# A block-sorted attention with a Fourier-mix layer: another order on all engines, one more pair of identity matmuls, and a buffer's clear on GpSimd

## The chip, the cores and the metric

The kernel runs on one core of a Trainium2 chip. A core has five instruction streams: PE (TensorE, matmuls and the weight loads PEld that go with them), DVE (VectorE), ACT (ScalarE), POOL (GpSimd) and SP (SyncE, which here only issues DMAs). They wait for each other through semaphores. The metric is device time in microseconds (us). Three runs of the kernel before gave 272.65 us in the median (271.55, 272.65, 272.99). The profile is of a further execution: 271.9 us as timed, with a span of 270.1 us from its first to its last instruction.

## The reference, cut to what matters

There are four batches of 8 heads, 768 positions and head size 64. For each head an 8x8 matrix is made doubly stochastic in five rounds, and mixes the eight 96-row blocks of K and V. Block-local attention follows. Its output, reshaped to 768x512 per batch, goes through a 2-D Fourier transform of which the real part is kept, a residual, a normalization and a two-layer MLP with 2048 hidden units.

```python
P = sort_net
for _ in range(5):
    P = np.exp(P - max(P, -1)); P = P / sum(P, -1); P = P / sum(P, -2)
k_sorted = einsum('bhij,bhjcd->bhicd', P, k_b); v_sorted = einsum(..., P, v_b)
scores = scale * q_b @ k_sorted.T          # inside each of the 8 blocks
attn = softmax(scores); x = attn @ v_sorted
u = x + real(fft2(x))                      # per batch, 768 x 512
un = (u - mean(u)) / sqrt(var(u) + 1e-6)
out = u + relu(un @ w_ch1) @ w_ch2
```

## The kernel before, in words

The program is cut into small steps, written as generators `t_<letter>`. A long string, `ORDER`, is a list of tokens; each token runs one generator up to its next `yield`. At the end every instruction of PE, DVE, ACT, SP and POOL is tied to the one before it on the same engine. So the string fixes the order on each engine, and only semaphores decide when an instruction starts. A second string, `SLOTS`, gives one digit to each buffer that is taken in that order: which of eight PSUM banks, or which copy of a rotating SBUF tile.

A token's letter names the step and its digits the batch, head pair, tile or column group. A trailing A or D says whether ACT or DVE empties PSUM, and a P or D whether POOL or DVE does an addition. The steps that matter here, with their lines:

- `M`: matmuls with the identity that sum V over the block rows (L425). `Z`: the mean from them (DVE L432, L437). `s`: V minus its mean, six DVE operations per V load (L463). `v`, `w`: V mixed by the stochastic matrix (L476, L486), copied out by ACT or DVE (L286, L288).
- `J`, `D`: the stochastic matrix spread over partitions by PE (L389, L448). `B`, `T`, `b`: its block-diagonal forms (DVE L398, L410, L452).
- `q`: Q transposed, for batches 0 and 1 by PE (L306), for 2 and 3 by a crossbar transfer: a DVE copy into the single buffer `qr` (L297), then a DMA transpose from SP (L300). `k`: K mixed (PE L511) and copied to one of two `ksb` buffers.
- `x`: scores (PE L529) and exp (ACT L534). `e`: exp minus 1 into one of four score buffers `ebuf` (DVE L548). `o`: attention times V (PE L561), reciprocal and product (DVE L570, L575).
- `a`, `A`, `R`, `r`: a correction for the means, to small tables (PE L583, L608, L615; ACT L627; DVE L636).
- `f`, `c`, `d`, `p`: the Fourier transform (DVE L680 to L707, PE L719, PE L755 and L758, DVE L769, ACT L776, POOL L782 and L784). `g`, `l`, `n`: normalization (DVE L791 and L795, POOL L799 to L808, ACT L816 or DVE L819), transposed by PE (L830) in batch 0 and by a DMA transpose (L825) in the others.
- `h`: first MLP layer (PE L843, relu by ACT L852 or DVE L850). `y`: second layer (PE L863), residual (DVE L868), output from SP (L870).
- `C`, `L`, `V`: loads. `C0` is a constant table, its copy into `vcx` by POOL (L357), then four loads of w1 (L362) and four of w2 (L365). `L20`, `L21`, `L30`, `L31` load Q, then K, of half a batch's heads (L188). `V` loads the second half of V (L229). All but the tables are issued by POOL, in its order.
- `I`: two 128x512 matmuls with the identity whose result nobody reads (L277), which wait for a given round of the stochastic iteration.

Ahead of the string come, in program order: the first loads from POOL (two of V, then Q, K, Q, K of batch 0), clears of buffers, and `load_next`, which loads Q and K of batch 1 (L203). Three of the four `ebuf` buffers are cleared by DVE (L246), the fourth by POOL (L258). The five rounds of the stochastic iteration (L316 to L324) run on DVE and ACT.

Of the kernel before, what the change touches and what calls it, by code (L numbers as in the profile page):

```python
# [18 lines left out]
H = 8  # L19
S = 768  # L20
D = 64  # L21
# [85 lines left out]
def kernel(  # L107
# [10 lines left out]
    nc = tc.nc  # L118
# [7 lines left out]
        "00011101 00010234 50671030 12436570 13541602 05240031 63725241 "  # L126
        "61012052 63475001 25314102 06103012 04513222 10030415 11274602 "
        "53130145 36510210 03210302 01560420 33200075 60111221 22340330 "
        "01276225 10173200 00200653 04210013 13610004 56102525 11621110 "
        "65112701 35471623 05243052 00016450 16110470 21112364 21160323 "  # L130
        "61172420 61372041 64161010 20345245 17630010 04176325 11271652 "
        "37261401 05032102 33560171 00310010 00620057 32036401 11017624 "
        "23213156 23520605 43101204 47051106 01110521 03411070 16502411 "
        "02713260 50732415 00274113 52224760 11003511 22104731 00001210 "
        "17315000 14236220 31041230 03107652 01103651 01547162 30400762 "
        "37631401 07521240 11101501 01641320 27614031 54302100 11023201 "
        "50262732 36000054 07001001 51143120 04353542 00117102 16572110 "
        "40111035 60270456 07453147 352041 "
# [27 lines left out]
    def start(ins):  # L166
        return tc.keep_in_program_order(ins)
# [74 lines left out]
    NE = 4  # L242
    eb4 = const.tile([97, NE, 2 * S], F16, name="eb4")
    ebuf = [eb4[:, n, :] for n in range(NE)]
    for n in range(NE - 1):
        nc.vector.memset(ebuf[n][0:96, :], 0.0)  # L246
# [11 lines left out]
    start(nc.gpsimd.memset(ebuf[NE - 1][0:96, :], 0.0))  # L258
# [621 lines left out]
    def t_i():  # L880
        idle_mm(1)
# [3 lines left out]
        "C0 I4 I5 M00 M01 M02 M03 J M04 M05 C0 B0 C1 B1 B2 D q00A Z0 "  # L885
        "Z0 s02 k00AA H k01AD Z0 s03 q00 k00 k00 k00 x001 k01 b0 s01 "
        "x000 x001 s04 b0 x000 x000 a0 a0 x001 s05 s00 q01D k01 q02D "
        "k01 k02AA q01 e001 k02 k02 v61A v61 v40A e001 v70A v40 v41D "
        "v50D a0 b1 k02 v41 q02 v30A v30 x010 V x010 x010 V T1 v70 "
        "v20A e010 v20 v50 e000 e000 e010 A0 R0 x011 x021 R0 R0 R0 "  # L890
        "q03D q03 R0 R0 x011 x011 x021 v60D v10A v60 v00A k10AA v10 "
        "e011 e011 x021 k03AA R0 v00 x020 x020 k03 k03 k03 o00 o01 "
        "k10 k10 k10 x020 e021 x030 o00 e020 x030 x030 e021 o02 o01 "
        "o00 o01 o03 o02 o03 x031 q11A r1 C2 C3 r0 r1 e030 o03 e020 "
        "o04 k11AA x031 e031 x031 o05 e030 R0 o04 e031 o04 q11 k11 R0 "
        "o02 o05 k11 q10A q13A q13 v51A o07 o07 o05 q10 v51 M10 o06 "
        "v31A k11 x111 x101 x101 x101 v31 M11 o07 o06 f00 o06 f00 "
        "v21A v01A f01 f01 k13AA e101 x110 f02 k13 f02 M12 M13 e101 "
        "f03 f03 M14 v21 x100 x111 x110 x111 e110 c00 L20 f04 x100 "
        "x110 c00 b1 L30 M15 C0 L20 q20 C0 f05 f05 Z1 v01 C0 e111 "  # L900
        "e110 c01 c01 c02 c00 e111 c01 c02 c03 c04 e100 r0 r0 v71A "
        "k12AA c03 q20 c04 d02 v71 v11A x100 d02 p02P d00 p02 d01 k12 "
        "q12A k12 e100 d00 c03 p00P p01P q12 v11 k13 d02 c04 d00 d01 "
        "Z1 c02 d04 p00 k12 k13 d01 p02 p01 p01 p04P Z1 I1 p00 d05 T2 "
        "g02 g01 p05P x121 x121 x131 x131 a1 o13 o10 a1 x121 g00 g01 "
        "x131 C0 g02 g00 l00 l00 l00 l00 e121 o12 I2 x130 e131 o11 "
        "d04 o12 d05 x130 x130 d05 d04 k20AA n001AA o11 q21 I3 e130 "
        "o11 d03 n001 n002AA n001 L21 n000DD o16 n002 p04 o12 n000 "
        "n000 L21 C0 p04 o16 p05 C0 n002 x120 x120 d03 k20 e130 p03P "
        "o13 s15 e120 o13 h00iA h00fD h00f h00i x120 o10 s10 o10 "  # L910
        "h00jD h00j e121 d03 h00cA h00pA h00hA h00h h00p q21 o16 "
        "h00dA e120 k21AA k21 s13 k21 k20 k20 h00c h00kD e131 s12 s14 "
        "x200 k21 h00oA h00nA s11 o14 x200 h00d x200 h00gA o17 h00aA "
        "h00k h00a h00lA wpA h00g p05 C0 o17 o17 o15 h00mA h00bA g05 "
        "o15 o14 o14 wkA h00l h00b wk h00n h00eA h00e o15 f10 h00o wp "
        "y0010 y0020 e200 g04 x201 x201 L30 x211 x211 p03 p03 g03 f11 "
        "f11 g04 f10 f12 h00m C0 g05 g03 l01 f12 e200 f13 y0021 y0022 "
        "l01 l01 x201 weD wbA wb wgD c10 we y0023 l01 q22 f13 n011DA "
        "e201 c10 f14 woA c11 c11 wo y0000 wjD e211 wj x211 y0001 "
        "n011 n011 c12 wg f15 whA wdA y0011 y0002 c13 c12 wh y0023 "  # L920
        "y0023 r1 n012DD f15 n012 y0012 wlA n012 c13 y0013 wcA q22 "
        "wnD waA wa n010DD n010 wl y0003 n010 wd c14 c14 h01aA wn "
        "y0003 wfD q23 q23 T3 y0013 c10 d11 h01oA h01o wiA h01dD h01d "
        "h01lA h01l y0003 y0013 d10 h01pA wc h01a wi h01p wf h01jD "
        "wmD h01gA wm e201 x210 d10 d10 c11 h01g x210 x210 p10P h01j "
        "d12 h01mA k22AD k22 k22 k22 e210 e210 k23DD q31 k23 k23 "
        "h01cA c13 d11 p12P h01c h01hA h01h p11P k23 h01fA h01f e211 "
        "h01iA d12 h01bD d12 p11 h01m h01i h01kA x230 x231 d11 h01b "
        "p12 p12 p11 g11 g12 g11 g12 x220 h01eA x230 h01e x220 x230 "
        "y0110 o22 x231 e231 o20 h01nD h01n o20 h01k o21 p10 p10 o23 "  # L930
        "o23 o20 L31 x220 L31 g10 g10 o23 y0111 y0112 y0120 a1 l10 "
        "l10 l10 l10 o22 o22 y0121 k31AA c14 n101A k31 q31 e230 e220 "
        "A1 c12 x231 o21 o21 k31 x221 n101 R1 e231 R1 n100A n100 "
        "y0100 y0101 q30 R1 R1 R1 n102A n102 x221 y0113 y0113 d13 "
        "y0102 y0122 R1 R1 e230 y0113 x221 e221 k31 d14 R1 R1 r2 r2 "
        "h10iA h10nA h10i d14 q30 k30DD e221 k30 k30 k30 y0123 r2 "
        "e220 y0123 p14P o27 h10eD h10n h10e h10kD o27 d14 y0123 "
        "y0103 d15 o27 h10aA h10a h10dA h10gA h10g h10bA y0103 h10k "
        "p13D p15P h10cA h10c h10hA h10mA h10m h10d q32 d13 d13 y0103 "
        "h10lA h10h h10jD p13 p14 p14 g14 d15 d15 g14 p15 p15 h10fA "  # L940
        "h10f h10oA o26 g15 p13 g13 g13 g15 l11 l11 l11 h10j o26 "
        "h10pD o26 h10b y1010 l11 o24 o24 y1000 h10l o25 n110D o25 "
        "h10o h10p y1011 x311 x311 x311 x301 f21 o25 f21 y1001 n112A "
        "x301 y1020 y1021 o24 f20 f20 n110 r3 e301 n111D y1002 y1012 "
        "f22 f22 f23 f23 c20 c20 y1013 y1022 q32 x300 x301 x300 x310 "
        "y1023 c21 c21 n112 f24 f25 c23 n111 e311 q33 y1013 y1023 c23 "
        "h11cD c22 f25 y1003 y1003 y1023 y1003 c22 c24 x300 h11c c24 "
        "k32DD k33DA k33 k33 e311 x310 k32 k32 d21 k33 p21P k32 d21 "
        "d21 e300 h11fD h11f h11oA e310 d22 d20 p20P h11lA p22P d22 "
        "d22 c24 h11mA c20 r3 h11kA q33 y1013 d20 h11l h11o p22 p22 "  # L950
        "h11m x310 h11hD h11jA h11j g22 o32 x331 e300 x331 h11bA p21 "
        "h11h x331 h11k g22 o32 h11eA h11iA e310 p20 c23 e301 p21 g21 "
        "h11b o32 h11pD h11aD h11a h11e h11i d20 p20 g20 g20 e331 "
        "x330 g21 l20 l20 l20 l20 h11p x321 h11gA h11g h11dA o31 x321 "
        "o30 o31 o31 e321 x321 h11nA h11d n202A y1110 x330 c22 o33 "
        "h11n y1111 y1112 n202 o33 e330 e331 c21 n201A o33 n201 n200D "
        "n200 r3 y1100 y1101 e321 x320 x320 e320 y1113 y1113 o30 "
        "y1120 x320 x330 e330 y1102 y1103 y1121 y1122 y1123 y1103 "
        "h20nA h20aA h20dD h20a d24 p24P y1123 y1123 d24 d24 d23 h20n "
        "h20lD h20l h20pD h20kD p23P h20k o30 h20jA h20j y1103 d25 "  # L960
        "d25 p24 p24 p25P g24 h20fD h20f h20p h20cA h20iD y1113 o34 "
        "h20c h20bA h20b h20eD d23 d23 d25 h20d p23 e320 h20mD o35 "
        "o35 h20i p25 p25 g25 o35 h20gA o37 h20hA p23 g23 g23 h20oA "
        "h20h h20g g25 h20e o36 o36 g24 l21 l21 l21 o36 l21 n210A "
        "h20o h20m o34 o37 o34 f30 f30 o37 y2020 y2010 y2021 y2022 "
        "y2011 f32 y2023 n210 y2012 y2013 f31 f31 f32 f33 f33 n212D "
# [75 lines left out]
```

## Time and profile before

| | busy us | share of the 270.1 us span | instructions |
|---|---|---|---|
| PE | 251.8 | 93% | 2440 |
| DVE | 196.3 | 73% | 489 |
| ACT | 126.0 | 47% | 287 |
| POOL | 75.0 | 28% | 118 |

The span is the measure to which durations of the trace are added up. A busy time is the union of an engine's instructions, so an engine can be busy and still be waiting in a part of the run where another engine sets the pace. Matmuls overlap, so that the mean of one (326 ns for 128x384) is longer than its share of PE's time (0.65 us for four of them in the chain of waits). The first MLP matmul (L843) starts at 61.84 us, and the last matmul of the second layer ends shortly before 267.4 us.

### The profile page before, as it was taken

What the parts mean: (1) busy time and instruction counts of PE and PEld (TensorE: products, weight loads), DVE (VectorE), ACT (ScalarE), POOL (GpSimd) and SP (SyncE); (2) the same over time, 40 slices, a digit from 0 to 9 for tenths busy, and PEclk for the clock granted to TensorE, in tenths of its full rate; (3) what the DMA queues carried; (4) which work ended last, traced back from release to release, by engine and by line L of the source; (5) the groups of instructions that cost most, each with busy time, mean ns of one, the idle gap of its engine ahead of it and who ended that gap; (6) DMA issues with size and microseconds to landing.
All of it is one profiled execution on the core that took longest, in us unless ns stands there. A gap on an engine that the chain in (4) does not pass through costs nothing.

```text
span 270.1 us, 6119 instructions
## 1 busy us (share of the span) xinstructions
PE 251.8 (93%) x2440; PEld 156.0 (58%) x2440; DVE 196.3 (73%) x489; ACT 126.0 (47%) x287; POOL 75.0 (28%) x118
## 2 busy tenths in 40 slices
PE   0789889789999999999999999999999999999995
PEld 0268776565666666655656655466466545545554
DVE  6787999989999677867698696458965825912523
ACT  2268889885575477352633555133314312431100
POOL 8922400578730006402220053024200521410000
PEclk9988999999999999999999999999999999999999
DMA  6999999989971231843022310230023023020006
GB/s 120 203 253 203 221 245 235 181 104 178 204 119 39 45 102 29 119 107 101 15 55 52 94 47 12 55 119 1 19 42 116 0 45 132 0 53 8 0 12 223
DMA packets 33138, 26.38 MB, mean 98 GB/s; under 512 B 17395, under 2 KB 28787, under 8 KB 33108
## 3 DMA queue, kind: packets, MB, share of 16 engines
q0 software_dynamic: 11712, 13.63, 30.4%
q1 hardware_dynamic: 21398, 12.36, 17.2%
q8 instruction: 19, 0.31, 0.5%
q14 instruction: 9, 0.07, 0.1%
HBM read 29.00 MB, written 6.29 MB: 131 GB/s over the span
## 4 chain that ended last, share of the span: by engine, by line
PE 77%; DVE 8%; DMA 8%; POOL 2%; ACT 2%; issue 1%; DVEq 0%; SPq 0%; POOLq 0%
PE pf L863 31%; PE pf L843 27%; DMA k<-in_k_dram 6%; PE pf L719 3%; PE pf L561 3%; PE pf L529 2%; DVE eb L548 2%; DMA out_dram<-u 2%; PE pf L755 2%; PE pf L758 1%; DVE u L769 1%; PE pf L486 1%; PE pf L511 1%; PE pf L476 1%; PE pf L615 1%
## 5 line engine op out<-in xcount | busy, mean ns | idle before, releaser
L843 PE MATMUL pf<-ut,w1sb 128*128 128x384 f16 x512 | 89.9, 326 | 0.4 <-DVE hr L850 0.2
L863 PE MATMUL pf<-w2sb,hr 128*128 128x512 f16 (+1 forms) x432 | 88.6, 355 | 0.0
L843 PEld LDWEIGHTS <-w1sb 128*128 128x128 f16 x512 | 48.7, 98 | 31.5 <-issue 0.4
L852 ACT ACTIVATE hr<-pf 128x384 f16<-128x384 f32 x78 | 35.8, 494 | 60.6 <-PE pf L843 60.5
L863 PEld LDWEIGHTS <-hr 128*128 128x128 f16 x432 | 38.5, 98 | 37.7
L782 POOL TENSOR_TENSOR u<-u,bs 128x255 f32<-128x255 f32 x21 | 17.6, 844 | 120.2 <-ACT bs L776 69.1
L868 DVE TENSOR_TENSOR u<-pf,u 128x512 f32<-128x512 f32 (+1 forms) x27 | 17.0, 628 | 29.0 <-PE pf L863 28.9
L534 ACT ACTIVATE ex<-pf 96x384 f32<-96x384 f32 x64 | 28.8, 490 | 10.6 <-PE pf L529 8.0
L850 DVE TENSOR_SCALAR hr<-pf 128x384 f16<-128x384 f32 x50 | 26.3, 547 | 7.7 <-PE pf L843 7.6
L548 DVE TENSOR_SCALAR eb<-ex 96x384 f16<-96x384 f32 x64 | 22.9, 374 | 2.6 <-ACT ex L534 2.4
L769 DVE SCALAR_TENSOR_TENSOR u<-r,pf 128x256 f32<-128x256 f16 x48 | 18.3, 411 | 6.6 <-ACT bs L776 3.2
L784 POOL TENSOR_TENSOR u<-u,bs 128x255 f32<-128x255 f32 x21 | 17.7, 849 | 6.5 <-DVE u L769 6.4
L816 ACT ACTIVATE un<-u,nm,ny 128x512 f16<-128x512 f32 x14 | 11.1, 810 | 17.2 <-POOL nm L808 13.5
L791 DVE BATCH_NORM_STATS2 st<-u 128x6 f32<-128x512 f32 x24 | 16.3, 688 | 3.5 <-POOL u L784 3.1
L286 ACT CAST vsf<-pf 96x512 f16<-96x512 f32 x23 | 16.4, 741 | 3.1 <-PE pf L486 3.1
L575 DVE TENSOR_TENSOR r<-pf,rz 128x384 f16<-128x384 f32 x32 | 17.3, 547 | 0.2
L561 PEld LDWEIGHTS <-eb 97*128 97x128 f16 x384 | 14.9, 97 | 3.7 <-DVE eb L548 0.5
L561 PE MATMUL pf<-vsf,eb 97*128 97x65 f16 x384 | 16.4, 194 | 0.3 <-ACT ex L534 0.2
L733 ACT ACTIVATE y<-pf 128x386 f16<-128x386 f32 x16 | 7.4, 498 | 11.3 <-PE pf L719 11.3
L529 PE MATMUL pf<-qt,ksb 64*128 64x96 f16 x256 | 10.0, 209 | 2.5 <-ACT ksb L286 1.9
L277 PE MATMUL pf<-pack 128*128 128x512 f16 x12 | 4.4, 458 | 8.4 <-DVE pw L324 8.2
L286 ACT CAST ksb<-pf 128x384 f16<-128x384 f32 x23 | 10.5, 484 | 2.3 <-PE pf L511 1.6
(118 smaller groups left out, 302.8 us busy)
## 6 DMA issues: line engine op xcount, KB each, us to landing
out_dram<-u SPq DMA_DIRECT2D x23, 256.0 KB, 2.3
vst<-in_v_dram POOLq DMA_DIRECT2D x4, 768.0 KB, 11.7
q<-in_q_dram POOLq DMA_DIRECT2D x6, 384.0 KB, 13.2
k<-in_k_dram POOLq DMA_DIRECT2D x6, 384.0 KB, 10.6
w1sb<-in_moe_w_ch_dram POOLq DMA_DIRECT2D x4, 512.0 KB, 18.6
w2sb<-in_moe_w_ch_dram POOLq DMA_DIRECT2D x4, 512.0 KB, 8.1
kq<-in_k_dram POOLq DMA_DIRECT2D x2, 384.0 KB, 15.1
kq<-in_q_dram POOLq DMA_DIRECT2D x2, 384.0 KB, 16.2
```

Source lines behind the costliest of these rows:

```text
L286: nc.scalar.copy(dst, src)
L534: nc.scalar.activation(ex.rearrange("p j (c r) -> p j c r", r=6), pss[h2][0:96].rearrange("p j (r c) -> p j c r", c=16), AF.Exp, scale=SCALE)
L548: nc.vector.tensor_scalar(ed, exs[b, hp, g, h2], -1.0, None, op0=ALU.add)
L561: nc.tensor.matmul(po[:, 65 * T:65 * T + 65], e[:, S * g + 256 * tt + 128 * n: S * g + 256 * tt + 128 * n + 128], vsf[:, vi:vi + D + 1], s ...
L575: nc.vector.tensor_tensor(rt[:, :, D * h:D * h + D], po3[:, :, 0:D], rz[:, :, None].broadcast_to([128, 6, D]), op=ALU.mult)
L769: nc.vector.scalar_tensor_tensor(u[:, o:o + 256].rearrange("p (j n) -> p j n", n=2), rts[b][:, T, o:o + 256].rearrange("p (j n) -> p j n", ...
L782: e.tensor_tensor(u[:, 1:256], u[:, 1:256], bs[:, 1:256], op=ALU.add)
L784: e.tensor_tensor(u[:, 257:512], u[:, 257:512], bs[:, 255:0:-1], op=ALU.subtract)
L843: nc.tensor.matmul(ps, w1sb[:, c, 128 * fc:128 * fc + 128], uns[b, g][:, c, :], start=(c == 0), stop=(c == 3))
L850: nc.vector.tensor_scalar(hr[:, fc, :], ps, 0.0, None, op0=ALU.max)
L852: nc.scalar.activation(hr[:, fc, :], ps, AF.Relu)
L863: nc.tensor.matmul(po, hrs[b, g][:, fc, 128 * tt:128 * tt + 128], w2sb[:, fc, cols], start=(fc == 0), stop=(fc == 15))
```

## The change

The order string is written anew, with the same steps in it and one more token, and the string of buffer digits with it. Seen by engine:

- POOL clears two of the four `ebuf` buffers and DVE two, instead of one and three.
- A new step `t_F` takes the place of `t_i`, which no token used. It issues two identity matmuls with no wait of their own. One token `F6` runs it, on PE between the correction step `a0` and the first K mixing. The tokens `I1` to `I5`, two matmuls each as before, stand at other places.
- PE begins with `M00` instead of `I4 I5`. DVE begins with the mean and the six subtractions of V, ahead of the block-diagonal forms.
- POOL's order of loads was: table copy, V, V, L20 (Q), L30 (Q), w1, L20 (K), w1, w1, then w1, L21 and w2 between POOL's additions and normalization steps. It becomes: table copy, V, w1, L20 (Q), V, w1, w1, L20 (K), w1, w2, and later w2, L30 (Q), w2, w2, L30 (K), L21 (Q), L21 (K). The DMA transposes of Q for batch 2 (`q20`, `q21`) come later and the other way round on SP.
- Some PSUM copies change engine. Over the program, ACT has 89 instead of 78 of the 128 relus, 28 instead of 23 of the 32 `ksb` copies and 7 instead of 10 of the 16 copies of `w`. DVE has 6 instead of 3 of the 24 pairs of additions of `p`, and 15 instead of 13 of the 30 normalizing operations and first-batch copies of `n`.

```diff
     SLOTS = (
-        "00011101 00010234 50671030 12436570 13541602 05240031 63725241 "
+        "00011101 01112340 56016704 56301701 25620421 73530212 01041030 "
...
-    for n in range(NE - 1):
+    for n in range(NE - 2):
         nc.vector.memset(ebuf[n][0:96, :], 0.0)
...
-    start(nc.gpsimd.memset(ebuf[NE - 1][0:96, :], 0.0))
+    for n in (NE - 2, NE - 1):
+        start(nc.gpsimd.memset(ebuf[n][0:96, :], 0.0))
...
-    def t_i():
-        idle_mm(1)
+    def t_F(n):
+        idle_mm(2)
...
     ORDER = (
-        "C0 I4 I5 M00 M01 M02 M03 J M04 M05 C0 B0 C1 B1 B2 D q00A Z0 "
-        "Z0 s02 k00AA H k01AD Z0 s03 q00 k00 k00 k00 x001 k01 b0 s01 "
-        "x000 x001 s04 b0 x000 x000 a0 a0 x001 s05 s00 q01D k01 q02D "
-        "k01 k02AA q01 e001 k02 k02 v61A v61 v40A e001 v70A v40 v41D "
-        "v50D a0 b1 k02 v41 q02 v30A v30 x010 V x010 x010 V T1 v70 "
...
+        "C0 M00 M01 I3 M02 M03 M04 I4 M05 J Z0 Z0 H Z0 s05 D s01 s00 "
+        "C1 q00D q01A b0 s03 B1 s02 s04 a0 F6 q00 q01 b0 a0 k01AA k01 "
+        "k01 B0 B2 b1 v50A v50 k01 v61D v40A v60D v41D v40 k00AA k00 "
+        "v60 x011 v61 x011 x011 k00 x010 x010 k00 v41 q03D k03AD q03 "
+        "x001 x000 e010 k03 x001 k03 v30D e011 e011 a0 k03 x000 x010 "
+        "e010 x000 e000 e001 x001 C0 e001 e000 v20A v70A V C0 v00A "
+        "v00 v70 v10A v20 A0 v30 T1 v10 x031 R0 x031 x031 R0 L20 V C0 "
+        "x030 o02 R0 R0 C0 L20 C0 C0 R0 o02 R0 x030 o03 o03 e031 e031 "
...
-        "o11 d03 n001 n002AA n001 L21 n000DD o16 n002 p04 o12 n000 "
-        "n000 L21 C0 p04 o16 p05 C0 n002 x120 x120 d03 k20 e130 p03P "
-        "o13 s15 e120 o13 h00iA h00fD h00f h00i x120 o10 s10 o10 "
...
+        "x120 l00 x121 l00 d04 p05P o12 o11 k20AA k20 d03 o12 k20 k20 "
+        "d03 o11 n002DA o11 o10 M15 Z1 p05 C0 n002 o10 n001AD n001 "
+        "o13 n000AA n002 n000 n000 n001 x130 o10 e131 q21 e131 k21DA "
+        "k21 k21 k21 x121 p03 p03 Z1 e120 L30 h00hA h00oA g03 p05 "
...
-        "y3103 y3122 y3123 y3123 y3123 I6 "
+        "I6 y3123 y3123 "
```

## The prediction

> **What bounds the kernel now.** I read the page's head first, then the busy time by stage with the granted clock, then the waits of PE, then the first 25 us in order of time. The head:
>
> ```profile
> span 270.1 us, 6119 instructions
> PE 251.8 (93%) x2440; PEld 156.0 (58%) x2440; DVE 196.3 (73%) x489; ACT 126.0 (47%) x287; POOL 75.0 (28%) x118
> ```
>
> PE is nearly full, but the mean hides two stages. The table by stage gives for each stretch its length, each engine's busy time with its instructions, the granted clock, the DMA share and GB/s:
>
> ```profile
> 11.60:18.40 6.80, 5.41 (x64) 3.67 (x62) 6.14 (x16) 4.01 (x9) 2.31 (x4) 1.00 1.29 228
> 18.40:21.80 3.40, 3.29 (x48) 2.71 (x48) 1.79 (x4) 2.93 (x10) 2.93 (x4) 0.50 1.23 252
> 21.80:25.00 3.20, 2.67 (x73) 2.47 (x74) 2.41 (x8) 2.21 (x5) 0.11 (x1) 0.99 1.31 203
> 25.00:30.00 5.00, 4.75 (x91) 4.35 (x91) 4.73 (x12) 4.61 (x12) 1.12 (x2) 1.00 1.29 216
> 30.00:61.84 31.84, 27.37 (x499) 20.14 (x494) 30.77 (x87) 27.78 (x67) 12.37 (x19) 1.00 1.05 190
> 61.84:267.40 205.56, 204.95 (x1672) 121.71 (x1671) 142.45 (x337) 81.86 (x183) 45.67 (x70) 1.00 0.31 69
> ```
>
> From the first MLP matmul (61.84 us) to the end of the last one PE is busy for 204.95 of 205.56 us; its waits there are two of 0.2 us. Nothing in that stretch can be gained but work taken off PE. From 30 to 61.84 us DVE is busy for 30.77 of 31.84: it sets the pace. Only before 30 us do both have holes: DVE idles 0.66 + 1.61 + 0.79 + 0.27 = 3.33 us between 11.6 and 30. The largest is where the clock is 0.50. What PE and DVE did around it:
>
> ```profile
> 16.16 0.53 PE L306 MATMUL pf<-pack,q 128*64 128x128 f16 x12
> 18.44 0.82 PE L529 MATMUL pf<-qt,ksb 64*128 64x96 f16 x16 [1.25 <-ACT ksb L286]
> 19.91 0.85 PE L306 MATMUL pf<-pack,q 128*64 128x128 f16 x12
> ...
> 21.13 0.56 DVE L288 CAST ksb<-pf 128x384 f16<-128x384 f32 x1 [1.61 <-PE pf L511]
> ```
>
> The same twelve transposes took 0.53 us and, at half clock, 0.85 us, and DVE sat 1.61 us behind them for a K tile. So the time is that of the first MLP matmul, plus PE's fixed 205.6 us, plus 2.7 us of last addition and output. The change must bring that first matmul forward or it brings nothing.
>
> **What the Trainium skill says.** "TensorE: Matmul & The Clock Gate", Part 1 (What's actually happening): PE runs at half rate until it was busy for a window of about 3.4 us, falls back after an idle one, and K is 4/8 or 8/8. The trace agrees: four 128x512 matmuls took 2.10 us from 8.15 us, four took 1.03 us from 11.79, and the half-rate stretch is 3.40 us long. The same page (Architectural detail) has ACT and DVE as strict FIFOs; hence the 1.61 us hold everything behind them. "DMA: Bandwidth & Descriptors" (Issuing engines are not separate DMA queues) says that DMAs of all issuers interleave on the same 16 engines. The eight transposes of Q land in 2.8 to 9.0 us, the long ones while loads run. "VectorE: DVE Perf Modes" (Zero memsets can be issued as uint32) halves a zero clear of f16 on DVE; here 0.70 us on DVE against 1.77 us on POOL.
>
> **The change, part by part.**
> *Clear.* DVE loses one of 0.70 us at 0.95 us. The stochastic iteration behind it starts at 3.19 us and could start when its input is there, about 2.4: 0.7 us earlier all along, to 11.7 instead of 12.4. POOL gains 1.77 us, which push the loads of batch 1 from 10.34 to 12.1 us. Their queue is backed up until the last K of batch 0 lands (22.3 us), and their data is first used at 29.8: hidden, 0.
>
> *V first.* PE's 16 matmuls M and I, 8.15 to 14.34 us now with J inside, come ahead of J. By the two paces (2.10/4 at first, 1.03/4 after 11.8) M ends at about 13.5 and DVE's first token starts at 13.8 instead of 13.40: +0.4 us, which uses up the 0.7. In exchange six subtractions (0.74 us each, 4.4 in all) stand ahead in DVE, where they wait for nothing more. Now they are spread from 15.6 to 19.5 us, and behind them DVE runs dry.
>
> *F6 and the moved I.* Two matmuls of 0.22 us each at full pace. They follow the correction matmuls, where PE waits for DVE's B1, s02 and s04 (1.9 us): hidden, bounds 0 and +0.43, I take 0.2. With two transposes, M, D and the correction in the same window PE has more work between 15 and 18.4 us than now, so the clock should stay at full. The bounds are a whole stretch removed (-1.6) and one left where it is (0). I5, I1 and I2 also stand before the first MLP matmul, as I1 to I3 do now: 0.
>
> *Work ahead of the first MLP matmul.* I counted both strings, with the page's mean for each instruction. PE 48.7 and 48.7 us (F6 and three K halves in, one o and one a out), DVE 55.5 and 55.6, ACT 49.7 and 48.2, POOL 19.6 and 16.3. So the order brings no lighter load there: only DVE's holes can move that matmul. The last of its operands needs DVE 52.7 us deep in its list now, 52.4 then.
>
> *Loads.* w1 is issued by about 23 us instead of 29.6 to 55.2, because L30's Q no longer waits 7.0 us in POOL's queue for its buffer. But w1 was there at 60.4 us for a use at 61.8, so this only permits an earlier start. The second half of V comes behind a w1 piece and a Q, at 42 instead of 37.5 us, and M13 wants it after 50: hidden. On POOL, p and l lose three loads from between them. The transpose of `q21` follows its copy as before, still beside four loads (w2, Q, K); at up to 9.0 us it frees `qr` about when DVE comes to `q20`'s copy: 0 to +0.7, I take 0. `q20` gets the loads of L21 behind it, and its scores come 10 us later: 0.
>
> *Engines of copies, buffer digits.* Whole program: DVE 213.8 to 211.7 us of row means, ACT 141.6 to 145.7, POOL 63.7 to 58.6. After 61.84 us DVE has 63 us to spare and ACT 124. The digits keep the same banks; an unlucky reuse could cost a few tenths: 0 to +0.7.
>
> *Tail.* I6 now stands before the last residual but still behind the last matmul: 0.
>
> *Sum.* -1.6 (half-rate stretch) - 0.8 (the hole at 21.8 to 25) + 0.4 + 0.2 = -1.8 us against the span of 270.1, or 268.3. The runs' median is 2.55 us above the span: 272.65 - 1.8 = **270.9 us**.
>
> **The rivals.**
> *The hole moves (no change).* DVE must still wait for the tables' correction: PE needs 2.5 us for A0 (L608, L615), then ACT's copy, and DVE's T1 may end 0.9 us before. And the third tile of the normalization now has its additions begun late on POOL (two of 0.85 us, after ACT's copy), 0.8 us short of DVE's list. 1.7 us would be handed back: 272.6. For it: ACT is busy for 27.8 of 31.8 us, so little else can fill in. Against it: DVE hides such waits today (1.07 us idle in 32).
>
> *A second half-rate stretch (slower).* PE's work before 61.84 us is of small matmuls with holes (27.37 busy of 31.84), which may fall below what keeps the clock. Each stretch cost DVE 1.6 us. One, as now, gives 272.65 + 0.4 + 0.2 = 273.3; two give 274.9. It decides from the second stretch on before the MLP, or from one plus a held `qr`. Against it: none came after 21.8 us before.
>
> *All holes close.* 3.33 - 0.4 = 2.9 us gained: 269.7, with PE's own waits a little shorter 269.4. It needs every load in time.
>
> *The change does not do what it says*: the pair lands outside the window and the stretch stays, 273.3; I count it with the second rival.
>
> **How the numbers follow.** A measurement of this kernel can tell about 0.5%, 1.36 us, from no change. Forecast 0.45 (of it 0.05 inside the band), all holes 0.07, hole moves 0.28, slower 0.20. Faster by over 0.5%: 0.40 + 0.07 = 0.47; within: 0.28 + 0.05 = 0.33; slower: 0.20. The forecast's own range is 270.0 to 271.9. For 8 in 10 I take 268.8 to 274.4: below, 269.4 with the runs' own spread of 0.7; above, most of the way to 274.9, with the unknown tenths of the buffers and `qr` in it.
>
> **What would show it.** Right: the clock at 1.00 from 12 us on; DVE's idle time from 12 to 30 us near 1 us; the first L843 near 60.0 us; from there PE again without waits over 0.3 us, for 205 to 206 us. Wrong in part: a 0.50 stretch elsewhere; DVE waiting at L636 or L791; the first L843 at 61 to 62 us. Wrong altogether: PE waits after the first L843, at score or relu buffers, or at a transpose's landing.

## The result and the profile after

The changed kernel takes 276.14 us in the median of four executions (275.49 to 276.33), against 272.10 us for the kernel before (271.47 to 272.99). The ratio is 1.0142 with a 95% interval of 1.0103 to 1.0181: it became 1.4% slower, where 270.9 us had been forecast, with 268.8 to 274.4 for eight cases in ten. Four more executions of the same kernel later gave 1.0184 (1.0130 to 1.0237). The profiled execution has a span of 273.7 us, 3.6 more than before.

Lines of the changed kernel have numbers one higher than before: L843 is L844 there. The head of the page after, with the span and the busy time of each engine:

```profile
span 273.7 us, 6108 instructions
PE 250.4 (91%) x2442; PEld 155.3 (57%) x2442; DVE 191.7 (70%) x483; ACT 129.6 (47%) x298; POOL 67.1 (25%) x113
```

PE does no more than before, and the span grew: the time went into waiting. The table by stage says where. Columns are as before: length of the stretch, busy time and instructions of PE, PEld, DVE, ACT and POOL, granted clock, DMA share, GB/s.

```profile
11.60:18.40 6.80, 6.37 (x63) 4.01 (x61) 4.39 (x10) 3.35 (x8) 3.92 (x7) 1.00 1.29 214
18.40:21.80 3.40, 2.35 (x59) 2.01 (x58) 3.40 (x8) 2.38 (x8) 1.69 (x4) 1.00 1.27 241
21.80:25.00 3.20, 2.44 (x71) 1.79 (x66) 3.20 (x9) 3.15 (x9) 1.64 (x3) 1.00 1.24 242
...
30.00:62.65 32.65, 26.95 (x488) 19.80 (x485) 29.44 (x83) 26.73 (x61) 10.58 (x17) 1.00 0.89 182
62.65:270.98 208.33, 204.67 (x1670) 121.96 (x1668) 138.71 (x333) 86.46 (x199) 37.49 (x63) 1.00 0.34 69
```

From 18.4 to 25 us it is what was forecast: the clock is 1.00, and DVE is busy for 3.40 of 3.40 and 3.20 of 3.20 us where it had idled 1.61 and 0.79. Ahead of that a new hole has opened. DVE's first token of the string, with the wait before it, in the kernel before and then in the changed one:

```profile
13.40 1.35 DVE L398 TENSOR_TENSOR bdk<-pf,pack 128x256 f16<-128x256 f32 x3 [0.46 <-PE pf L389]
...
14.50 0.69 DVE L433 TENSOR_REDUCE vb<-pf 128x64 f32<-128x512 f32 x1 [2.31 <-PE pf L426]
```

DVE now begins with V's mean, and waits 2.31 us until PE has summed V. From 12 to 30 us it idles 2.85 us (18.00 less 15.15 busy), against 3.26 before, and not the forecast "near 1 us". So less was gained early than it looks. And the first MLP matmul comes at 62.65 us, not at 60.0 and not even at the old 61.84. And from there PE is no longer without waits: 204.67 us of work take 208.33, where 204.95 had taken 205.56. PE's waits, summed over the run (the longest, 9.0 us for the first data of V, is left out):

```profile
PE pf L720 <- DMA cs<-k_cs: 1.5, 1, 1.5
PE pf L864 <- DVE hr L851: 1.5, 1, 1.5
PE pf L562 <- DVE r L576: 1.2, 1, 1.2
PE pf L759 <- DMA rb<-rr: 1.1, 1, 1.1
...
PE pf L844 <- DVE u L770: 0.9, 1, 0.9
```

These are three places. The first lies ahead of the MLP: PE waits for `cs`, the large table of the Fourier step, at 42.5 to 44 us, and for `rb`, a small one, at 49.4 to 50.5. `cs` was issued at 34.59 us and landed at 43.84; before it was issued at 34.81 and landed at 41.41, and nothing waited for it.

The second is at 71 us. DVE's and then PE's part of the timeline (start, duration, engine, line, tiles; in brackets the idle time before it and what ended it):

```profile
70.38 0.56 DVE L851 TENSOR_SCALAR hr<-pf 128x384 f16<-128x384 f32 x1
73.54 0.36 DVE L298 COPY qr<-q 128x768 f16<-128x768 f16 x1 [2.61 <-DMA qt<-qr]
73.82 0.55 DVE L851 TENSOR_SCALAR hr<-pf 128x384 f16<-128x384 f32 x1
...
74.42 1.02 PE L864 MATMUL pf<-w2sb,hr 128*128 128x512 f16 x4 [1.48 <-DVE hr L851]
```

The copy for `q20` goes into the single buffer `qr`. It waits until the transpose of `q21`, issued at 62.90 us, has read it, at 73.52. A relu stands behind the copy on DVE, and the second MLP layer needs it.

The third is at 120 to 137 us. SP's issues in the timeline of the changed kernel:

```profile
119.54 0.52 SPq L871 DMA_DIRECT2D out_dram<-u  x1
120.41 1.19 SPq L826 DMA_TRANSPOSE ut<-un  x1
122.79 1.21 SPq L301 DMA_TRANSPOSE qt<-qr  x1
124.05 0.58 SPq L664 DMA_DIRECT2D rb<-rr  x1
124.68 0.59 SPq L871 DMA_DIRECT2D out_dram<-u  x1
```

What DVE waited for in that stretch:

```profile
121.76 0.42 DVE L770 SCALAR_TENSOR_TENSOR u<-r,pf 128x256 f32<-128x256 f16 x1 [1.99 <-DMA out_dram<-u]
127.03 0.42 DVE L770 SCALAR_TENSOR_TENSOR u<-r,pf 128x256 f32<-128x256 f16 x1 [1.22 <-DMA out_dram<-u]
130.96 0.75 DVE L770 SCALAR_TENSOR_TENSOR u<-r,pf 128x256 f32<-128x256 f16 x2 [2.65 <-DMA out_dram<-u]
```

There are six buffers `u`, and each Fourier result of batch 1 takes the one of a tile of batch 0 that must first be written out. The sum of the second of these tiles (L869) was done at 118.4 us, but SP issued its output at 124.68, behind two transposes and a small table. So DVE stood for 5.9 us in three waits, and PE ran dry twice behind it: 0.93 us up to 131.76 (L844 in the list above) and 1.19 us up to 137.03 (L562).

### The profile page after: what moved, and what is told of

Its sections match the earlier page's. It is cut to its first block, busy times and chain, and to the rows that moved or that the text cites. A ratio compares the mean times of both kernels' runs of the same rounds, so it can differ in the third digit from the quotient of the medians.

```text
span 273.7 us, 6108 instructions
## 1 busy us (share of the span) xinstructions
PE 250.4 (91%) x2442; PEld 155.3 (57%) x2442; DVE 191.7 (70%) x483; ACT 129.6 (47%) x298; POOL 67.1 (25%) x113
## 4 chain that ended last, share of the span: by engine, by line
PE 69%; DMA 16%; DVE 8%; ACT 2%; SPq 2%; issue 1%; POOL 1%; DVEq 0%; ACTq 0%; POOLq 0%
PE pf L864 29%; PE pf L844 23%; DMA qt<-qr 4%; DMA vst<-in_v_dram 4%; DMA cs<-k_cs 3%; PE pf L720 3%; PE pf L562 3%; DMA rb<-rr 2%; DMA out_dram<-u 2%; PE pf L530 2%; DVE u L770 1%; PE pf L512 1%; PE pf L759 1%; PE pf L756 1%; PE pf L487 1%
## 5 line engine op out<-in xcount | busy, mean ns | idle before, releaser
L844 PE MATMUL pf<-ut,w1sb 128*128 128x384 f16 x512 | 90.1, 326 | 0.9 <-DVE u L770 0.9
L844 PEld LDWEIGHTS <-w1sb 128*128 128x128 f16 x512 | 49.0, 98 | 32.9 <-DVE u L770 1.3
L853 ACT ACTIVATE hr<-pf 128x384 f16<-128x384 f32 x89 | 40.3, 494 | 49.1 <-PE pf L844 48.7
L783 POOL TENSOR_TENSOR u<-u,bs 128x255 f32<-128x255 f32 x18 | 13.4, 744 | 125.5 <-ACT bs L777 93.4
L869 DVE TENSOR_TENSOR u<-pf,u 128x512 f32<-128x512 f32 (+1 forms) x27 | 16.6, 626 | 22.7 <-PE pf L864 22.5
L851 DVE TENSOR_SCALAR hr<-pf 128x384 f16<-128x384 f32 x39 | 20.8, 550 | 9.2 <-PE pf L844 8.6
L549 DVE TENSOR_SCALAR eb<-ex 96x384 f16<-96x384 f32 x64 | 21.9, 365 | 0.9 <-ACT ex L535 0.8
L562 PE MATMUL pf<-vsf,eb 97*128 97x65 f16 x384 | 16.0, 194 | 1.5 <-DVE r L576 1.2
L562 PEld LDWEIGHTS <-eb 97*128 97x128 f16 x384 | 14.6, 97 | 4.9 <-DVE r L576 1.6
L287 ACT CAST vsf<-pf 96x512 f16<-96x512 f32 x19 | 13.3, 729 | 6.8 <-PE pf L487 5.8
L426 PE MATMUL pf<-vst,pack 128*128 128x512 f16 x24 | 8.1, 439 | 9.1 <-DMA vst<-in_v_dram 9.0
L777 ACT COPY bs<-pf 128x256 f32<-128x256 f32 x24 | 8.6, 374 | 15.9 <-PE pf L759 12.4
L817 ACT ACTIVATE un<-u,nm,ny 128x512 f16<-128x512 f32 x12 | 9.8, 813 | 10.6 <-DMA ut<-un 6.3
L820 DVE TENSOR_SCALAR un<-u,ny,nm 128x512 f16<-128x512 f32 x12 | 6.7, 576 | 10.4 <-POOL nm L809 6.4
L287 ACT CAST ksb<-pf 128x384 f16<-128x384 f32 x28 | 13.1, 488 | 1.8 <-PE pf L512 1.6
L785 POOL TENSOR_TENSOR u<-u,bs 128x255 f32<-128x255 f32 x18 | 13.6, 758 | 0.0
## 6 DMA issues: line engine op xcount, KB each, us to landing
kq<-in_k_dram POOLq DMA_DIRECT2D x2, 384.0 KB, 13.8
```

The costliest lines, as they stand in the source:

```text
L287: nc.scalar.copy(dst, src)
L549: nc.vector.tensor_scalar(ed, exs[b, hp, g, h2], -1.0, None, op0=ALU.add)
L562: nc.tensor.matmul(po[:, 65 * T:65 * T + 65], e[:, S * g + 256 * tt + 128 * n: S * g + 256 * tt + 128 * n + 128], vsf[:, vi:vi + D + 1], s ...
L844: nc.tensor.matmul(ps, w1sb[:, c, 128 * fc:128 * fc + 128], uns[b, g][:, c, :], start=(c == 0), stop=(c == 3))
L851: nc.vector.tensor_scalar(hr[:, fc, :], ps, 0.0, None, op0=ALU.max)
L853: nc.scalar.activation(hr[:, fc, :], ps, AF.Relu)
```

## The experiments

The table holds every kernel that ran, in the order of the text. "First" is the start of the first MLP matmul in the profiled execution, "rest" the time from there to the end of the last matmul. The digits for buffers move with their tokens.

| kernel | ratio to before (95%) | median us | first | rest |
|---|---|---|---|---|
| before | 1 | 272.1 | 61.84 | 205.6 |
| changed | 1.0142 (1.0103 to 1.0181) | 276.14 | 62.65 | 208.3 |
| a_same (changed, again) | 1.0184 (1.0130 to 1.0237) | 277.26 | 62.94 | 208.4 |
| a_tab | 1.0030 (1.0011 to 1.0048) | 272.75 | 60.95 | 207.1 |
| a_w1 | 1.0070 (1.0048 to 1.0093) | 273.54 | 60.10 | 211.2 |
| a_qr | 1.0063 (1.0044 to 1.0082) | 273.98 | 62.54 | 205.3 |
| a_qt | 1.0072 (1.0043 to 1.0102) | 273.96 | 63.53 | 205.1 |
| a_out | 1.0058 (1.0043 to 1.0073) | 273.45 | 64.47 | 205.5 |
| a_all | 0.9886 (0.9853 to 0.9918) | 269.05 | 59.58 | 203.9 |
| a_all2 (the same) | 0.9883 (0.9864 to 0.9902) | 268.74 | 60.27 | 204.4 |
| a_all_nof | 0.9929 (0.9898 to 0.9960) | 270.03 | 61.02 | 204.4 |
| a_all_nof2 (the same) | 0.9917 (0.9900 to 0.9935) | 269.69 | 60.76 | 203.9 |
| a_all_clr | 0.9882 (0.9856 to 0.9908) | 268.55 | 61.72 | 203.9 |
| a_nof | 1.0114 (1.0084 to 1.0144) | 275.51 | 62.51 | 208.6 |
| b_pair | 0.9981 (0.9968 to 0.9994) | 271.61 | 62.78 | 205.3 |
| b_clear | 1.0005 (0.9985 to 1.0024) | 272.32 | 63.00 | 205.4 |
| b_tab | 1.0020 (0.9996 to 1.0044) | 272.37 | 61.89 | 205.2 |

The executions of the changed kernel's variants spread over about 3 us (a_qr: 271.85 to 275.6), so that one profiled execution need not be the median's (a_qr's took 272.3). The ratios come from all executions, "first" and "rest" from the profiled one. Some of these hold a stretch at half clock that others don't: a_same, a_tab, a_qr, a_qt and a_all_clr one between 35 and 48 us, a_out two of them from 43.7 to 50.6, a_w1 one from 74.2 to 77.6; the kernel before, b_pair, b_clear, a_all_nof and a_all_nof2 have theirs between 16 and 27. So the late "first" of a_out or a_qt is not the work of their edits alone, and the ratios decide.

### The changed kernel once more

> The changed kernel as it is, once more beside the others, so that their differences are against more than four runs of it: 276 us, ratio 1.014 to 1.016. If its executions spread over 3 us as those of its variants did, the median may lie up to 1 us lower.

It took 277.26 us. The loss is there in both series; the gains below are given against the smaller one, 1.0142, whose interval is about 1.1 us to either side. Against 1.0184 each of them would be 1.1 us larger.

### Place one: the tables

```diff
-        "v00 v70 v10A v20 A0 v30 T1 ... o01 C2 x021 C3 q10A ..."
+        "v00 v70 v10A v20 C2 C3 A0 v30 T1 ... o01 x021 q10A ..."
```

> The changed kernel, with one edit: the loads of the tables cs, lt and the row of rb are tied to an earlier DVE instruction (about 26 us instead of 34.6), with the same order on SP. My theory: PE's waits for cs (1.46 us) and for rb (1.1 us) between 42 and 51 us handed back what the early stage had gained; with cs there by about 38 us both go, the first matmul of the MLP comes 1.5 to 2.0 us earlier than 62.65 us, and the time falls by as much, to 274.1 to 274.6. Rival A: DVE sets the pace of this stage and had work for nearly all of it, so the first MLP matmul comes at most 0.5 us earlier. Rival B: the tables take the place of V and Q in the loads' queue, and PE then waits for those: 0 or slower.

`cs` was issued at 26.86 us and landed at 35.99. Both waits are gone and the first MLP matmul came at 60.95 us, 1.7 earlier. The time fell by (1.0142 - 1.0030) x 272.1 = 3.0 us, more than the 1.5 to 2.0 expected. My theory holds, both rivals fall. But by the profile the tables account for 1.7 us of it. The other 1.2 lie behind the first MLP matmul ("rest" of 207.1 instead of 208.3), where PE's wait at place two is the same 1.5 us and those at place three are 0.7 us in place of 2.1; the section on place three comes back to it.

Why was the table late? a_w1 leaves the table where it is and moves only POOL's loads.

```diff
-        "... V C0 v00A ... L20 V C0 ... R0 C0 L20 C0 C0 R0 ... C2 x021 C3 ..."
+        "... V v00A ... L20 V ... R0 L20 R0 ... C2 x021 C3 C0 C0 C0 C0 C0 ..."
```

> The changed kernel, with one edit: on POOL the four loads of w1 and the first of w2 go behind V, Q, V and K of their stretch, so that w1 is issued from about 29 us on instead of 21 to 30. The tables are tied to the same DVE instruction as in the changed kernel. My theory: the early w1 loads are what delays cs (landed at 43.8 us against 41.4 in the kernel before, for issues at 34.6 and 34.8): cs lands by 41.5 us, PE's wait for it falls under 0.3 us, and 1 to 2 us are gained. Rival: the loads are backed up to 55 us in any order and the table shares the engines with whatever is in flight, so cs lands within 1 us of 43.8 and the time stays within 0.5 us of 276.1 to 277.3.

The DMA view of the changed kernel, issues from 34 to 45 us (tile, engine, number, KB each, median us to landing):

```profile
cs<-k_cs SPq DMA_DIRECT2D x1, 579.0 KB, 9.3
```

The same view of a_w1:

```profile
cs<-k_cs SPq DMA_DIRECT2D x1, 579.0 KB, 7.0
```

With w1 behind V, Q and K the table landed at 41.37 us, PE did not wait for it, and the first MLP matmul came at 60.10 us. So POOL's new order of loads had made SP's table late. The Trainium skill says how such a thing is possible ("DMA: Bandwidth & Descriptors", Queues, rings and completion order): each of the DMA engines takes its queues in turn, a packet at a time. The landing times fit that. While `cs` was in flight, GpSimd's queue moved 1.56 MB in the changed kernel, 0.96 MB in a_w1 and 0.87 MB in the kernel before, where `cs` took 9.3, 7.0 and 6.6 us. What in a load of w1 takes a larger part than a load of Q was not tried.

a_w1 shows something else as well. It gained 2.0 us, but in the profiled execution the first MLP matmul came 2.55 us earlier and PE's end 0.3 us later. From its timeline of PE:

```profile
73.01 1.02 PE L864 MATMUL pf<-w2sb,hr 128*128 128x512 f16 x4 [2.61 <-DVE hr L851]
...
75.65 1.90 PE L864 MATMUL pf<-w2sb,hr 128*128 128x512 f16 x4
```

The wait at place two grew from 1.48 to 2.61 us: a wait for a transfer that lands at its own time takes back a part of what was gained ahead of it. And just behind that wait the clock fell to one half, from 74.2 to 77.6 us: four matmuls that had taken 1.02 us took 1.90, and PE's busy time from the first MLP matmul on is 206.20 us against 204.67. This execution took 275.75 us. Twelve of the sixteen kept a clock of 0.999 or 1.00, with a median of 273.50, so most did not lose this second part.

```diff
-        "v20A e010 v20 v50 e000 e000 e010 A0 R0 ... q11A r1 C2 C3 r0 r1 ..."
+        "v20A e010 v20 v50 e000 e000 e010 C2 C3 A0 R0 ... q11A r1 r0 r1 ..."
```

> The kernel before, with one edit: its tables cs, lt and rb are tied to an earlier DVE instruction (about 25 us instead of 34.8), as in the changed kernel's experiment. There PE waits for no table, so my theory is no change: ratio 0.998 to 1.002. Rival: DVE and PE wait for the tables in a way that the profile puts down to other releasers, or other loads come later: 1 us either way.

`cs` was issued at 28.10 us and landed at 37.38. The edit did what was expected, nothing that can be told: 1.0020, with the first MLP matmul at 61.89 us.

### Place two: the transpose of `q21`

```diff
-            qr = wt([128, 6, 2, D], F16, "qr", 1)
+            qr = wt([128, 6, 2, D], F16, "fo" if (b, hp) == (2, 1) else "qr", 1)
```

> The changed kernel, with one edit: the copy of Q for q21 goes into another buffer (that of fo, unused from about 50 to 77 us) instead of the single qr. My theory: DVE's copy for q20 waited 2.61 us at 70.9 us for q21's transpose to land, the relu behind it on DVE held PE for 1.48 us, and nothing later gave that back. Then DVE's wait is gone, PE's wait on the relu is gone, and the time falls by 1.5 us, from 276.1 to about 274.6 (ratio to the kernel before 1.009). Rival A: the PE wait is only moved to the next thing that DVE or a late load of w2 brings (DVE idles elsewhere anyway): the copy no longer waits, but the time stays within 0.4 us of 276.1. Rival B: the transpose's slow landing itself is what matters, since its scores need it: no change either.

DVE's copy and PE's second layer in the timeline of a_qr:

```profile
70.75 0.52 DVE L298 COPY qr<-q 128x768 f16<-128x768 f16 x1
...
72.67 1.03 PE L864 MATMUL pf<-w2sb,hr 128*128 128x512 f16 x4
```

Neither waits any more, though the transpose still landed at 73.42 us, 10.6 us after its issue. The time fell by (1.0142 - 1.0063) x 272.1 = 2.1 us, where 1.5 had been expected. Rivals A and B fall.

```diff
-        "... M14 o12 g00 ... e131 q21 e131 ... x130 q21 h00l ..."
+        "... q21 q21 M14 o12 g00 ... e131 e131 ... x130 h00l ..."
```

> The changed kernel, with one edit: q21's copy on DVE and its transpose on SP go about 6 us earlier, to a stretch where the loads have run dry (57 to 60 us), with the single qr kept. It tells whether the transpose took 10.6 us because of the loads issued around it. My theory: it lands in about 3 us, as transposes with nothing beside them do (2.7 us at 91.7 us), q20's copy does not wait, and the time falls as with the second buffer, by about 2 us (ratio 1.006 to 1.009). Rival A: the transpose is slow whatever is beside it: lands after 66 us or more, though still before the copy of q20 comes. Rival B: DVE's 0.34 us in front of the first MLP matmul cost as much, or the wait turns up elsewhere: less than 1 us gained.

The transposes' time to landing, from the view of the tile `qr` of the changed kernel (60 to 80 us):

```profile
DMA to landing us min/median/max: 10.6/10.6/10.6
```

The same view of a_qt (50 to 80 us):

```profile
DMA to landing us min/median/max: 2.8/2.8/2.8
```

The same 192 KB took 2.8 us in the gap of the loads and 10.6 us among three loads of w2 and one of Q. Issued at 62.90, it was done at 73.52, 1.3 us ahead of the load issued 0.16 us after it (74.78). The gain is (1.0142 - 1.0072) x 272.1 = 1.9 us. My theory holds.

### Place three: outputs behind transposes

```diff
-        "q31 n101 y0110 d15 y0103 o22 o22 y0123 o22 ... q30 n100 q30 ... r2 y0103 o21 ... o20 r2 r2 o20 h10b o21 y0113 y0113 o21"
+        "q31 y0123 n101 y0110 d15 y0103 o22 o22 o22 ... q30 y0103 n100 q30 ... r2 o21 ... o20 o20 h10b o21 y0113 y0113 r2 r2 o21"
```

> The changed kernel, with one edit: on SP, the outputs of batch 0's tiles 5, 3 and 4 go ahead of transposes and small table copies that stand in front of them (T5 ahead of n101's transpose, T3 ahead of n100's, T4 ahead of r2's second and third). Nothing else moves. My theory: DVE's waits for u buffers at 119.8 to 131.0 us (1.99, 1.22 and 2.65 us, 5.9 in all) come from outputs issued up to 6 us after their sums were there, and cost PE 0.93 us at the first MLP layer and 1.19 us at the attention product: these go, and the time falls by 2.0 us to about 274.1 (ratio 1.007). Rival: the longest of the three waits is for one late packet of an output that was issued promptly (the other fifteen of its queues had landed 2 us before), so that an earlier issue takes away the first two waits (DVE only) and of PE's 2.1 us at most half: 0.5 to 1.0 us.

One wait for an output is left in DVE's timeline, and PE is busy for 12.00 of 12.00 us from 118 to 130 and from 130 to 142:

```profile
122.64 0.42 DVE L770 SCALAR_TENSOR_TENSOR u<-r,pf 128x256 f32<-128x256 f16 x1 [1.19 <-DMA out_dram<-u]
```

The time fell by (1.0142 - 1.0058) x 272.1 = 2.3 us; the theory said 2.0. The rival had something in it: in the changed kernel fifteen of sixteen queues of the third output were done by 128.75 us, and the last packets came at 130.83. Such a late part is in four of the seven profiles with the old order on SP, where DVE's third wait is 2.3 to 2.8 us; in the other three (a_tab, a_qr, a_qt) that wait is 1.0 us. None of the six profiles with the new order has it: there SP issues the third output 0.03 us after its sum, and not 1.48. Whether the new order keeps the late part away, or it was only absent, is not shown. So a part of the 2.3 us, and of the 3.0 of a_tab, may belong to it.

### All three

The edits of a_tab, a_qr and a_out together, in two series.

> The changed kernel with the three edits together: tables tied to an earlier DVE instruction, q21's copy in a buffer of its own, outputs of batch 0's second half ahead on SP. Alone they gave -3.0, -2.1 and -2.3 us against the 1.0142 of the changed kernel. My theory: they are three separate waits, so the gains add up to about -7, at most limited by what the early stage has gained: ratio 0.992 to 0.995 of the kernel before, 269.5 to 270.4 us. Rival: what was gained alone is partly the same (the kernels' executions spread over 3 us with the loads' landing times): the sum is about half, and the time that of the kernel before, 271.5 to 272.5.

> The changed kernel with the three edits together, once more, with more executions: ratio 0.988 to 0.990 of the kernel before, clock mostly 1.00.

The ratios are 0.9886 and 0.9883: 7.0 us less than the changed kernel, where the three alone add up to 3.0 + 2.1 + 2.3 = 7.4, and 3.1 us less than the kernel before, faster than the range that I had expected. The rival, half of the sum, falls. How exactly the gains add up depends on the base: against 1.0184 the three alone are 10.9 us and together 8.1, so that some overlap is possible. This version beats both kernels. The stage behind the first MLP matmul is without waits again, in the table by stage of a_all:

```profile
59.58:263.51 203.93, 203.93 (x1671) 121.88 (x1668) 139.05 (x333) 86.28 (x199) 37.62 (x63) 1.00 0.37 70
```

It is also shorter than in the kernel before: 203.9 to 204.4 us in the five profiles with the three edits, 205.2 to 205.6 in the four of the kernel before and its variants. Some 1.3 us of the 3.1 therefore lie here, where the prediction saw nothing to gain. The new order has moved three halves of K's mixing ahead of the first MLP matmul, where PE has holes: behind it the traces show 75 of these matmuls in place of 90, busy for 2.9 in place of 4.3 us. No run has tried this part alone.

### What the rest of the gain is made of

> The kernel before, with one edit: four identity matmuls (0.22 us each at full clock) on PE where it waits 1.25 us for ACT's copy of K at 17.2 to 18.4 us. They cost PE nothing there. My prediction's first step, by itself: the clock stays at 1.00 from 18.4 to 21.8 us, DVE's 1.61 us behind PE goes, and the time falls by 1.6 us, ratio 0.994. Rival: the stage after it (DVE busy 30.8 of 31.8 us, waits for loads that land when they land) takes it back: the clock stays up, the first MLP matmul comes less than 0.5 us earlier, ratio 0.998 to 1.000. Second rival: the clock falls all the same, since other windows decide: no change.

```diff
-        "... k00 k00 k00 x001 k01 b0 s01 ..."
+        "... k00 k00 k00 i i i i x001 k01 b0 s01 ..."
```

The time fell by 0.5 us (0.9981), not by 1.6, as the first rival had it. Every execution has a mean granted clock. One of the Trainium skill's windows of 3.4 us at half rate ("TensorE: Matmul & The Clock Gate", Part 1) takes 0.6% off that mean over 270 us, so that 0.994 means one such stretch; the 3.40 us measured before agree. Eighteen of twenty executions of b_pair show 0.999 or 1.00, with a median of 271.57 us. The kernel before, over 133 executions, shows the price directly: 48 at 0.999 or 1.00 have a median of 271.53 us, 29 at 0.994 have 271.59, and 56 at 0.987 or less, two stretches and more, have 272.44. By these medians one half-rate stretch costs this kernel 0.1 us. The profile of b_tab agrees: its clock stays at 1.00 without any pair, and its first MLP matmul comes at 61.89 us, that of the kernel before, with the stretch, at 61.84. b_clear's profile suggests why.

```diff
-    for n in range(NE - 1):
+    for n in range(NE - 2):
         nc.vector.memset(ebuf[n][0:96, :], 0.0)
...
-    start(nc.gpsimd.memset(ebuf[NE - 1][0:96, :], 0.0))
+    [start(nc.gpsimd.memset(ebuf[n][0:96, :], 0.0)) for n in (2, 3)]
```

> The kernel before, with one edit: two score buffers are cleared by POOL and two by DVE, as in the changed kernel. My prediction: the stochastic iteration starts up to 0.7 us earlier, POOL's loads of batch 1 are issued 1.3 to 1.8 us later, which nothing waits for: 0 to -0.7 us, ratio 0.9975 to 1.000. Rival: the loads' later issue moves the loads behind them and the tables that compete with them, so that PE waits: +0.3 to +1.

The ratio is 1.0005. Its profiled execution had a clock of 1.00 up to 22.6 us (and one half-rate stretch after that), so that it shows what the stretch of the kernel before hides. PE's timeline of the kernel before:

```profile
22.32 0.53 PE L511 MATMUL pf<-bdk,k 128*64 128x128 f16 x12 [0.60 <-DMA k<-in_k_dram]
```

That of b_clear:

```profile
19.91 0.53 PE L306 MATMUL pf<-pack,q 128*64 128x128 f16 x12
22.33 0.57 PE L511 MATMUL pf<-bdk,k 128*64 128x128 f16 x12 [1.90 <-DMA k<-in_k_dram]
```

At full clock PE reached that K tile 1.3 us earlier, and went on at 22.33 instead of 22.32 us, because the last K of batch 0 lands at 22.28 us. The half-rate stretch lay beside a load.

The added pair taken out, alone and with the three edits:

```diff
-        "... s04 a0 F6 q00 q01 b0 ..."
+        "... s04 a0 q00 q01 b0 ..."
```

> The changed kernel without the token F6, that is without the added pair of identity matmuls (0.43 us of PE at full clock). If the pair is what keeps the clock at full between 18 and 22 us, a stretch at 0.50 comes back there, DVE waits behind PE by about 1.6 us, and the first MLP matmul comes later than 62.65 us by up to 1.6. If the order alone (M's matmuls, D and the corrections closer together) keeps the clock up, nothing returns, and the time is the same or 0.2 us less.

Without the pair the changed kernel is at 1.0114 against 1.0142 with it: the intervals overlap, and with the three waits in place nothing can be told. Nor does the pair decide the clock there: one of the four executions without it, the profiled one, is at 1.00, and two of the eight with it.

> The changed kernel with the three edits together and without the added pair of identity matmuls. If the pair keeps the clock up where it stands, the clock of more executions falls to 0.994 and 0.987 and the time rises by 0.2 to 0.8 us over the 269.05 us of the three edits with the pair (0.9886); if it does nothing, the time stays within 0.3 us or falls by 0.2.

> The same without the added pair of identity matmuls. If the pair is worth what the clock's half-rate stretch costs, the clock falls in most executions and the time is 0.5 to 1.5 us above that with the pair. Rival: the pair does nothing, and the early gain comes from the order of DVE's work alone: within 0.3 us of it.

Without the waits the pair's worth can be told. Two rows of the table by stage with the pair, of a_all; the clock is third from the end:

```profile
18.40:21.80 3.40, 2.22 (x62) 1.99 (x60) 3.40 (x7) 2.20 (x6) 2.29 (x4) 1.00 1.23 271
21.80:25.00 3.20, 2.43 (x72) 1.93 (x69) 3.20 (x9) 3.15 (x9) 1.16 (x3) 1.00 1.28 210
```

The same rows without the pair, of a_all_nof:

```profile
18.40:21.80 3.40, 2.33 (x47) 2.20 (x47) 3.09 (x7) 2.37 (x8) 1.70 (x4) 0.74 1.27 243
21.80:25.00 3.20, 2.82 (x62) 2.05 (x61) 2.51 (x5) 2.66 (x7) 1.52 (x3) 0.74 1.24 241
```

Without the pair the clock falls to one half for about 3.4 us around 21.8, and DVE idles 0.31 + 0.69 us beside it. All twelve executions without the pair have a clock of 0.994 or less; seven of nine with it are at 0.999 or 1.00. The medians are 269.83 and 268.76: the pair is worth 1.1 us in this order, its own time included.

> The changed kernel with the three edits, and with three score buffers cleared by DVE and one by POOL as in the kernel before. In the kernel before, the clear on POOL changed nothing (ratio 1.0005), so I expect 0 to +0.5 us. Rival: with V's mean first in DVE's order the stochastic iteration is what DVE waits for, and 0.7 us of DVE ahead of it cost 0.7 us.

With three clears on DVE again (the edit of b_clear, undone) the ratio is 0.9882, against 0.9883: the clear does nothing here either. With 1.1 us for the pair and some 1.3 behind the first MLP matmul, about 0.7 of the 3.1 us is left for the order of V's mean and subtractions and the rest of the string together; it was not split further.

## Why the prediction was wrong, step by step

- *The bound* held as a form: start of the first MLP matmul, then PE's work, then 2.7 us (270.98 to 273.7). What failed is "PE's fixed 205.6 us". Full PE time before does not say that nothing can be lost: "rest" became 208.3. Nor was it fixed the other way: without the three waits it is 203.9 to 204.4. The "three K halves in" had been counted, and given no price.
- *Loads*, "hidden", failed. The step looked at each load that was moved and its own first use. It did not look at `cs` and `rb`, which were not moved but share the engines with what was. Measured: 2.6 us of PE's waiting, 3.0 us in time (a_tab, of which the start of the MLP is 1.7), and a_w1 gives back 2.0 by the loads alone. In a_all the start is at 59.58 us (a second execution: 60.27), where "near 60.0" was forecast.
- *The transpose of `q21`*, "0 to +0.7, I take 0", was mis-sized. The place was right, but the price came from the longest landing seen before, 9.0 us, and not from how many loads would now stand beside it: it was 10.6 us, DVE waited 2.61, the time grew by 2.1 us.
- *SP's order* had no term at all; the "0 to +0.7" next to it was meant for buffer digits. Each issue of a transpose held SP for about 1.2 us (1.19 and 1.21 above), and outputs that free a `u` stand behind. Measured: 2.3 us, which may hold a late part of an output.
- *The half-rate stretch and F6*, -1.6 and +0.2: the stretch went, as forecast, but its price was wrong. In the kernel before it is worth 0.1 us by the executions, and the wait for K that ends at the same time accounts for it; the step priced DVE's hole by what stood in front of it and not by what would end it next. In the changed kernel nothing waits for that K (it landed at 20.96 us), and with the waits gone the pair brings 1.1 us (a_all against a_all_nof), near to the 1.4 of the two terms. That is luck as far as the price goes, since it was read off a place where it does not hold. One more thing in this step differs from the traces: by the Trainium skill ("TensorE: Matmul & The Clock Gate", Part 1) the half rate comes back after an idle window, but it came back at 18.43 us in the kernel before and at 20.02 in a_all_nof, though PE was busy for 2.17 and 1.73 of the 3.41 us ahead.
- *V first*, DVE at 13.8 us: 14.50 in the changed kernel's profile, 13.79 in a_all, 14.82 in a_all2. What differs is the pace of PE's sums of V: in a_all four of these matmuls took 1.02 us from 11.86 us on, in a_all2 six took 2.98 us from 10.83 on, though the second half of V landed at 11.82 and 11.90 us. The sign "near 1 us" of idle time did not fit this step to begin with: DVE is done with what stands ahead at 12.2 us, and a start at 13.8 leaves 1.6 us of waiting. So the hole at 21.8 to 25 us, -0.8, did close, and another opened at 12.2.
- *The clear* was right for POOL, at 0 (b_clear, a_all_clr), and for the iteration, which ended 0.7 us earlier (its last step on DVE began at 11.71 instead of 12.41). *The tail* at 0 was right too: 2.7 us in both.
- None of the three rivals was it. The slower one came nearest: it named a held `qr`, and further half-rate stretches ahead of the MLP do come in some executions (in a_same's profile at 43.7 to 47.1 us, beginning in PE's wait for `cs`). But the two executions of the changed kernel at full clock took 275.49 and 276.19 us, so these stretches are not the cause. The line "wrong altogether" named the places, but had no chance and no size. A rival of the form "an earlier start meets transfers that land when they land" would have ended on the slower side.

Together: the kernel without the three waits is 3.1 us faster than the one before, and 3.0 + 2.1 + 2.3 us for the waits make 4.3 us slower, where 1.0142 - 1 is 3.9 us of 272.1 and the later series 5.0. The interval of the changed kernel alone is about 1.1 us to either side, and a_tab and a_w1 show that what one edit does moves the waits at the other places, so that the split between the three is not finer than that.

## What to carry to other kernels

When an order over all engines is rewritten, price each engine's queue, not only the moved steps: for each buffer with one copy or few, ask which transfer frees it, what stands ahead of that transfer on its queue, and what will be in flight beside it. A hole in a profile is worth what lies between its end and the next thing that would end it, so look for the wait that ends nearly at the same time. And when a rewritten order is slower, look for the two or three waits it has created before discarding it: here 7 us of them hid a gain of 3.

## What the runs showed of the hardware that was not expected

- A crossbar transpose of 128x768 16-bit elements lands in 2.8 us alone and in 10.6 us among loads that GpSimd issued, about when the loads issued beside it land.
- A 579 KB table from SP lands in 6.6, 7.0 or 9.3 us, by which of GpSimd's loads are in flight (0.87, 0.96 and 1.56 MB of them meanwhile), with the engines about as full in all three.
- One half-rate stretch of 3.4 us costs 0.1 us in one order of this program, and in another the pair of matmuls that keeps it away brings 1.1 us.
- Of an output's sixteen queues one can end 2.1 us after the others (128.75 and 130.83 us), in four of seven profiles of one order, and a buffer's next writer waits for the last.
